# Later loads held behind a cast, w_out ahead of B and C, weights cast on GpSimd and PSUM taken anew for the decays, in a fused state-space and GELU kernel

## Chip, core and metric

The kernel runs on one core of one Trainium2 chip. The metric is device time in microseconds (us) of one execution. Three executions of the kernel before took 119.41, 119.84 and 119.67 us, median 119.67 us. The profiled execution took 119.88 us, of which the profile shows a span of 118.2 us from the first to the last instruction.

## What is computed

The reference is a chunked state-space layer (Mamba-2 style) whose output goes through a GELU feed-forward layer. `x` is 4 x 8 x 768 x 32 (batch, heads, time, head width), `a` is 4 x 8 x 768, `B` and `C` are 4 x 8 x 768 x 16. Cut to what matters:

```python
for c in range(nc):                     # chunks of time, state carried along
    cum = cumsum(log(clip(a)))          # in the chunk
    M = (C @ B.T) * exp(cum_i - cum_j) * causal
    y = M @ x + (C @ state) * exp(cum)
    state = exp(cum_end) * state + sum_j B_j x_j exp(cum_end - cum_j)
h = y.reshape(3072, 256) @ w_in         # 256 x 2048
out = gelu_tanh(h) @ w_out              # 2048 x 256
```

All inputs and the output are float32. The kernel's matrix products run on bfloat16 copies.

## The kernel before

**Tiling.** The 3072 tokens are cut into 12 units of 256 tokens; a batch has three units. A unit holds two chunks of 128 tokens (numbered `gc`), one on each half of the partitions. Work for a unit goes through these steps, each a small function that issues instructions:

- `f_mul` (line 345, DVE) multiplies the unit's B and C by decay factors, one instruction each. Units 3 and later take the factors from a table that comes from `f_RTN` (line 288; its products are on line 280, PE), which the copies `f_rn` and the reciprocals `f_pn` turn into factors.
- `f_T` (line 366, PE) transposes B and C of units 0 to 3; the others are transposed by DMA (`f_XT`, line 355). `f_E` copies the transposes out of PSUM, on the engine that `PET` names. `f_F` (line 390, DVE) makes the two masked copies `ce` of C.
- `f_G` (line 406, PE) forms C times B in two PSUM tiles, the gram. `f_M` (line 416, DVE, two instructions a unit) masks it causally. For units below `VIA` the second half is first copied to SBUF by ACT (`f_gc`, line 412).
- `f_D` (line 456, PE) forms the sums that update the state, in a quarter of two PSUM banks; `f_S` (lines 482, 484) takes them out, and `f_SP` (line 500, DVE) spreads the state over a mask. For the first chunk `f_SP0` (line 493) does this on GpSimd (POOL).
- `f_session` (lines 430 and 441, PE) forms y of the unit. From unit `MERGE` to the last but one it also issues the next unit's `f_D` and `f_G`. `f_yev` copies y to the bfloat16 tile `xm`.
- `f_s1` (line 518, PE) is the first product of the feed-forward layer: eight groups of four matmuls a unit, two groups per quarter of w_in. `f_gelu` (line 526, ACT) follows each group. `f_s2` (line 535, PE) is the second: for each of the unit's two chunks four groups of four matmuls, one group per quarter of w_out. `f_oev` and `f_store` take the result out.

**Loads.** w_in and w_out come in four quarters of 512 KB each and are cast to bfloat16 by the helper on lines 257 to 261 (`copy`), on the engines in `WENG`; "POOL+POOL" is two casts of half a quarter. A unit's x is 256 KB, its B and its C 128 KB each. ACT's queue issues B of unit 0, C of unit 1, the first w_in quarter, B of unit 1 and the other w_in quarters. SyncE's queue (SP) issues everything else, in the order of `HEAD` and then unit by unit. Before the first of the later loads, C of unit 2, stands a gate: `f_gate` (line 160) lets POOL write one element of the target tile after an instruction of ACT (`ce` of unit 0), and the load, which overwrites that element, waits for it.

**Order.** Each engine executes its instructions in one fixed order. The order is made on the host by a planner (`run_order`, line 33): steps have an engine, an estimated duration, predecessors and a priority, and at each moment the engine that is free first takes the ready step of lowest priority number. DVE and POOL may hold back for a more urgent step that is nearly ready. PSUM is planned too: the four banks `bk` are taken by a step and given back when its readers are done; the gram has two tiles of its own. Where the plan shows PE waiting in the first 20 us, it fills the wait with matmuls of zeros (line 820). The estimates are numbers in the code; if a load really comes later than planned, the engine that waits for it still waits in its place in the order.

The names that the change touches: `WP`, `MERGE`, `PET`, `LI`, `LO`, `HEAD`, `WENG`, `PP`, `RP`, `XP`, `D1`, `VIA` (lines 552 to 577), `load_h` (line 617), the gate (lines 158 and 699), `Gn` and `Mn` (lines 728 and 742), and the fills (line 818).

## Time and profile before

| | |
|---|---|
| median of three executions | 119.67 us (119.41 to 119.84) |
| profiled execution | 119.88 us |
| span in its profile | 118.2 us |
| PE busy | 110.3 us, 93% |
| ACT busy | 72.3 us, 61% |
| DVE busy | 62.6 us, 53% |
| POOL busy | 32.5 us, 27% |
| read from and written to memory | 10.58 MB, 3.15 MB |

The profile lists instructions with start and duration in us from the start of the span, with the line of the kernel (a helper's line where a helper issues them), output and input tiles. PE is TensorE's matmuls, "PEld" its weight loads; "SPq" and "ACTq" are the queues that issue DMAs. An entry in square brackets is the idle time of the engine just before, and what ended it. The chain is the sequence of work that ended last, followed back from the last instruction.

### The profile page before, as it was taken

What the parts mean: (1) busy time and instruction counts of PE and PEld (TensorE: products, weight loads), DVE (VectorE), ACT (ScalarE), POOL (GpSimd) and SP (SyncE); (2) the same over time, 40 slices, a digit from 0 to 9 for tenths busy, and PEclk for the clock granted to TensorE, in tenths of its full rate; (3) what the DMA queues carried; (4) which work ended last, traced back from release to release, by engine and by line L of the source; (5) the groups of instructions that cost most, each with busy time, mean ns of one, the idle gap of its engine ahead of it and who ended that gap; (6) DMA issues with size and microseconds to landing.
All of it is one profiled execution on the core that took longest, in us unless ns stands there. A gap on an engine that the chain in (4) does not pass through costs nothing.

```text
span 118.2 us, 3828 instructions
## 1 busy us (share of the span) xinstructions
PE 110.3 (93%) x1631; PEld 93.6 (79%) x1631; DVE 62.6 (53%) x134; ACT 72.3 (61%) x154; POOL 32.5 (27%) x61
## 2 busy tenths in 40 slices
PE   5999979999999999999999999999999999999930
PEld 5867747778888888888888888888888888888820
DVE  2779598597495791923954917609429045000110
ACT  0543796656469495684693874956847938668300
POOL 7936954572531113103301114211011010000000
PEclk9999999999999999999999999999999999999995
DMA  3999999999999984947436991371011011020120
GB/s 69 187 273 328 325 279 310 256 181 220 199 138 207 99 140 50 214 102 132 137 46 98 205 186 53 82 64 56 31 44 44 6 44 44 6 92 0 44 92 6
DMA packets 46850, 15.04 MB, mean 127 GB/s; under 512 B 42320, under 2 KB 45232, under 8 KB 46832
## 3 DMA queue, kind: packets, MB, share of 16 engines
q1 hardware_dynamic: 41760, 9.93, 48.2%
q10 hardware_dynamic: 4208, 2.49, 7.7%
q0 software_dynamic: 864, 2.36, 7.2%
q8 instruction: 13, 0.21, 0.8%
q14 instruction: 5, 0.04, 0.1%
HBM read 10.58 MB, written 3.15 MB: 116 GB/s over the span
## 4 chain that ended last, share of the span: by engine, by line
PE 77%; DMA 8%; SPq 7%; DVE 1%; POOL 1%; issue 1%; ACT 0%; DVEq 0%
PE bk L535 35%; PE bk L518 31%; DMA wf<-in_moe_w_out_dram 6%; SPq L253 5%; PE bk L441 3%; PE gb L406 3%; SPq L167 2%; DMA a_t<-in_a_dram 2%; PE bk L430 2%; PE bk L456 1%; PE gb L280 1%; POOL w_out_sb L259 1%; DVE r_t L275 1%; PE bk L820 1%; PE bk L366 0%
## 5 line engine op out<-in xcount | busy, mean ns | idle before, releaser
L526 ACT ACTIVATE gT<-bk 128x512 bf16<-128x512 f32 x96 | 51.3, 600 | 11.5 <-PE bk L518 11.4
L518 PE MATMUL bk<-xm,w_in_sb 128*128 128x256 bf16 x384 | 49.1, 274 | 1.0 <-POOL w_in_sb L259 0.7
L535 PE MATMUL bk<-w_out_sb,gT 128*128 128x256 bf16 x384 | 49.7, 273 | 0.4 <-POOL w_out_sb L259 0.2
L518 PEld LDWEIGHTS <-w_in_sb 128*128 128x128 bf16 x384 | 37.2, 98 | 6.6 <-POOL w_in_sb L259 0.9
L535 PEld LDWEIGHTS <-gT 128*128 128x128 bf16 x384 | 36.7, 98 | 6.7 <-issue 2.5
L416 DVE TENSOR_TENSOR m<-gb,tri 128x1024 bf16<-128x1024 f32 x22 | 26.7, 1218 | 1.1 <-PE gb L406 1.1
L549 POOL DMA_DIRECT2D out_dram<-o_sb x18 | 9.9, 552 | 50.6 <-ACT o_sb L542 50.6
L257 ACT ACTIVATE xm<-bk 128x256 bf16<-128x256 f32 x22 | 7.4, 381 | 12.6 <-PE bk L456 8.0
L484 DVE SCALAR_TENSOR_TENSOR s_new<-s_new,pend,bk 128x64 f32<-128x64 f32 x16 | 4.4, 275 | 20.1 <-ACT xm L257 19.5
L542 ACT ACTIVATE o_sb<-bk 128x256 f32<-128x256 f32 x22 | 8.5, 386 | 8.8 <-ACT xm L257 4.7
L345 DVE TENSOR_TENSOR bc<-bc,fac 128x256 bf16<-128x256 f32 x24 | 10.6, 477 | 0.1
L500 DVE SCALAR_TENSOR_TENSOR sp_new<-s_new,pend,bmask 128x256 bf16<-128x256 f32 x19 | 9.2, 517 | 0.0
L259 POOL CAST x<-x_t 128x512 bf16<-128x512 f32 x12 | 7.7, 638 | 4.0 <-DMA x_t<-in_x_dram 3.4
L820 PE MATMUL bk<-wz 128*128 128x128 bf16 x59 | 7.2, 312 | 1.3 <-DVE warm L193 1.3
L544 DVE COPY o_sb<-bk 128x256 f32<-128x256 f32 x2 | 0.8, 424 | 14.0 <-PE bk L535 14.0
L820 PEld LDWEIGHTS <-wz 128*128 128x128 bf16 x59 | 6.1, 148 | 1.9 <-DVE warm L193 1.3
L390 DVE TENSOR_SCALAR ce<-bt,par 128x256 bf16<-128x256 bf16 x22 | 6.3, 337 | 1.6 <-ACT bt L257 1.6
L259 POOL CAST w_in_sb<-wf 128x512 bf16<-128x512 f32 (+1 forms) x7 | 5.0, 739 | 2.7 <-DMA wf<-in_moe_w_in_dram 2.7
L482 DVE COPY s_new<-bk 128x64 f32<-128x64 f32 x3 | 0.7, 225 | 9.2 <-ACT xm L257 5.1
L406 PE MATMUL gb<-ce,bt 32*64 32x256 bf16 x192 | 5.3, 291 | 0.1
L441 PE MATMUL bk<-m,x 64*32 64x128 bf16 x384 | 5.2, 226 | 0.0
L259 POOL CAST w_out_sb<-wf 128x1024 bf16<-128x1024 f32 (+1 forms) x4 | 3.8, 954 | 2.8 <-DMA wf<-in_moe_w_out_dram 2.8
(62 smaller groups left out, 50.5 us busy)
## 6 DMA issues: line engine op xcount, KB each, us to landing
x_t<-in_x_dram SPq DMA_DIRECT2D x12, 256.0 KB, 4.9
out_dram<-o_sb POOLq DMA_DIRECT2D x18, 128.0 KB, 2.8
wf<-in_moe_w_in_dram ACTq DMA_DIRECT2D x4, 512.0 KB, 7.5
wf<-in_moe_w_out_dram SPq DMA_DIRECT2D x4, 512.0 KB, 7.9
bc<-in_C_dram SPq DMA_DIRECT2D x11, 128.0 KB, 4.1
bc<-in_B_dram SPq DMA_DIRECT2D x10, 128.0 KB, 4.1
out_dram<-o_sb SPq DMA_DIRECT2D x6, 128.0 KB, 1.7
bc<-in_B_dram ACTq DMA_DIRECT2D x2, 128.0 KB, 5.2
```

Source lines behind the costliest of these rows:

```text
L259: nc.gpsimd.tensor_copy(out=o, in_=i)
L345: nc.vector.tensor_tensor(out=d["bc16"][:, i], in0=d["bc"][:, i].rearrange("p h (r n) -> p r h n", r=2), in1=f.rearrange("p r (h o) -> p r ...
L406: nc.tensor.matmul(out=GB[g // 2][ks, g % 2, 256 * r:256 * r + 256], lhsT=d["bt"][gs, 0, r, ks], rhs=ce[gs, :, :, ks], start=True, stop=Tr ...
L416: nc.vector.tensor_tensor(out=state[("m", u, f)].rearrange("p g r e t -> p g (r e t)"), in0=state.pop(("gc", u, f), gram[f]).rearrange("p ...
L441: nc.tensor.matmul(out=y[k][32 * q:32 * q + 32, w * Q:(w + 1) * Q], lhsT=X16[u][ks, r, 32 * h:32 * h + 32], rhs=m[w][ks, q // 2, r, q % 2, :],
L500: nc.vector.scalar_tensor_tensor(out=sp_new.rearrange("p (g d) -> p g d", g=4), in0=state[("s", gc)].rearrange("p (o d) -> p o d", o=1).to ...
L518: nc.tensor.matmul(out=hp[:, j * nt:(j + 1) * nt], lhsT=w_in_sb[:, kc, fi * 128:(fi + 1) * 128], rhs=xm[:, kc, c0 * Q:c0 * Q + nt], start= ...
L526: nc.scalar.activation(gts[g][:, i * per:(i + 1) * per, 0:nt], hps.pop((g, i)).rearrange("p (j t) -> p j t", j=per), AF.Gelu_apprx_tanh)
L535: nc.tensor.matmul(out=ops[gc], lhsT=gts[g][:, fi, tt * Q:(tt + 1) * Q], rhs=w_out_sb[:, fi, :], start=(fi == 0), stop=(fi == NF - 1), ski ...
L542: nc.scalar.activation(o_sb, ops.pop(gc), AF.Copy)
L549: q.dma_start(out=out[u * W:(u + 1) * W].rearrange("(p r) m -> r p m", r=2)[r], in_=ops.pop(gc))
L820: nc.tensor.matmul(out=BK[j][:, 0:128], lhsT=wz[:, 0:128], rhs=wz[:, 0:128], start=True, stop=True)
```

## The change

- **Hold and order of loads.** The gate moves from C of unit 2 to the first w_out quarter, which is now the first of the later loads. POOL writes the element with a memset, after the cast of the first w_in quarter. The order after the gate was C of unit 2, w_out 0, B of unit 2, w_out 1, 2, 3, x of unit 2. It is now w_out 0, w_out 1, C of unit 2, w_out 2, B of unit 2, w_out 3, x of unit 2.
- **Casts.** Every w_in quarter is one cast on POOL; so is the third w_out quarter, which was shared with DVE. The fourth stays shared.
- **Units 1 to 3.** `f_G` and `f_D` of unit 3 become steps of their own (`MERGE` 3), with two banks for `f_D`. `f_D` of unit 1 no longer waits for the fourth first product of unit 0. The masking of unit 1 reads PSUM directly (`VIA` 1). Unit 2's transposes are copied by ACT. `f_mul` of unit 1 gets a more urgent priority, the cast of its x, `f_G` of unit 1 and the products of `f_RTN` less urgent ones.
- **Planner.** The DMA estimates change, and all loads share one planned DMA resource.
- **Fills.** Zeros are multiplied in matmuls of 256 columns instead of pairs of 128.

```diff
+    def f_gate(kind, j):
+        if kind == "wo":
+            WF[("o", j)] = wfp.tile([128, 4, d_model], FP32, name="wf")
+            o = WF[("o", j)][0:1, 0, 0:1]
...
+        nc.gpsimd.memset(o, 0.0)
...
-    WP = (-185, -184.9, -179.5, -179.4)
-    MERGE = 2
+    MERGE = 3
-    PET = {0: "ACT", 1: "ACT", 2: "DVE", 3: "ACT"}
-    LB, LX, LI, LO, XD, XL = 0.92, 1.25, 1.85, 1.65, 0.6, 3.6
-    HEAD = [("x", 0, 2.6, 0), ("x", 1, 4.5, 0), ("b", 1, 1.1, WP[0]), ("wi", 1, 1.7, WP[1]),
-            ("wi", 2, 1.6, WP[2]), ("wi", 3, 1.6, WP[3]),
-            ("c", 2, 2.8, 0), ("wo", 0, 1.5, 0), ("b", 2, 0.85, 0), ("wo", 1, 1.5, 0), ("wo", 2, 1.5, 0),
-            ("wo", 3, 1.5, 0), ("x", 2, 1.15, 0)]
-    WENG = [("POOL", "POOL+POOL", "POOL+POOL", "POOL+POOL"), ("POOL", "POOL", "POOL+DVE", "POOL+DVE")]
+    PET = {0: "ACT", 1: "ACT", 2: "ACT", 3: "ACT"}
+    LB, LX, LI, LO, XD, XL = 0.92, 1.25, 1.42, 1.5, 0.6, 3.6
+    HEAD = [("x", 0), ("x", 1), ("b", 1), ("wi", 1), ("wi", 2), ("wi", 3), ("wo", 0), ("wo", 1), ("c", 2), ("wo", 2), ("b", 2), ("wo", 3), ("x", 2)]
+    SEND = {("b", 1): -185, ("wi", 1): -184.9, ("wi", 2): -179.5, ("wi", 3): -179.4}
+    WENG = [("POOL", "POOL", "POOL", "POOL"), ("POOL", "POOL", "POOL", "POOL+DVE")]
-    PP = -45
-    RP = 4
-    XP = {0: -96, 1: -7.5}
-    D1 = 3
-    VIA = 2
+    PP = -58
+    RP = 2000
+    XP = {0: -96, 1: 10}
+    GS = 0
+    D1 = None
+    VIA = 1
...
-    bl[1, 1] = add("DW", 5.2, none, done=1.35, prio=-2)
-    win_l[0] = add("DW", DW * 1.8, none, done=1.35, prio=-1)
+    bl[1, 1] = add("DMA", 1.4, none, done=1.35, prio=2.2)
+    win_l[0] = add("DMA", DW * 1.45, none, done=1.35, prio=2.4)
...
-        n = add("DW" if side else "DMA", DW * dur if side else DF * dur, none, deps=[lat], done=1.35, prio=10 + k)
+        n = add("DMA", DF * dur, none, deps=[lat], done=1.35, prio=2.1 if k == 5 else 10 + k)
...
-            issue["c", 2].deps.append(add("POOL", 0.15, f_gate, 2, 1, 0, deps=[fn_[1]], prio=-98))
...
-            Gn[u] = add("PE", 0.37, f_G, u, prio=(-87, -62)[u] if u < 2 else q, deps=Fn[u] + Mn.get(u - 1, []))
+            Gn[u] = add("PE", 0.37, f_G, u, prio=(-87, 900)[u] if u < 2 else q, deps=Fn[u] + Mn.get(u - 1, []))
...
-                             prio=q + 1 + r if u > 1 else (-60.3, -45.5)[u] + 0.1 * r))
+                             prio=q + 1 + r if u > 1 else (-60.3, -48)[u] + 0.1 * r))
...
+    held = HEAD[max(n for n, e in enumerate(HEAD) if e in SEND) + 1]
+    issue[held].deps.append(add("POOL", 0.1, f_gate, *held, deps=[SPn[0] if GS else wi_n[0][-1]], prio=-98))
...
-            for _ in range(n):
-                nc.tensor.matmul(out=BK[j][:, 0:128], lhsT=wz[:, 0:128], rhs=wz[:, 0:128],
+            for i in range(0, n, 2):
+                w = 128 * min(2, n - i)
+                nc.tensor.matmul(out=BK[j][:, 0:w], lhsT=wz[:, 0:128], rhs=wz[:, 0:w],
                                  start=True, stop=True)
```

More of the change, by code (lines that the diff above doesn't have):

```diff
@@ L156 @@
     P = [dict() for _ in range(NP)]
-    def f_gate(j, i, u):
-        P[j]["bc"] = ldn.tile([128, 2, H, 2 * N], FP32, name="bc")
-        nc.gpsimd.tensor_copy(out=P[j]["bc"][0:1, i, 0, 0:1], in_=P[u]["ce"][0:1, 1, 0:1])
+    def f_gate(kind, j):
+        if kind == "wo":
+            WF[("o", j)] = wfp.tile([128, 4, d_model], FP32, name="wf")
+            o = WF[("o", j)][0:1, 0, 0:1]
+        elif kind == "x":
+            XF[j] = ldx.tile([128, H, 2 * D], FP32, name="x_t")
+            o = XF[j][0:1, 0, 0:1]
+        else:
+            P[j]["bc"] = ldn.tile([128, 2, H, 2 * N], FP32, name="bc")
+            o = P[j]["bc"][0:1, "bc".index(kind), 0, 0:1]
+        nc.gpsimd.memset(o, 0.0)
     def load_bc(j, i, q):
@@ L173, in load_x @@
         b, t = divmod(j, T3)
-        XF[j] = ldx.tile([128, H, 2 * D], FP32, name="x_t")
+        if j not in XF:
+            XF[j] = ldx.tile([128, H, 2 * D], FP32, name="x_t")
         q.dma_start(out=XF[j], in_=x[b, :, t * W:(t + 1) * W].rearrange("h (p r) d -> p h (r d)", r=2))
@@ L251, in load_wo @@
     def load_wo(q, e):
-        WF[("o", q)] = wfp.tile([128, 4, d_model], FP32, name="wf")
+        if ("o", q) not in WF:
+            WF[("o", q)] = wfp.tile([128, 4, d_model], FP32, name="wf")
         e.dma_start(out=WF[("o", q)], in_=wo[:, 4 * q:4 * q + 4])
@@ L641 @@
             if key not in bl and key not in xl:
-                load_h(kind, j, LX if kind == "x" else LB)
+                load_h(kind, j)
     wdur = {"DVE": 0.68, "ACT": 1.08, "POOL": 1.08}
```

4 lines of the change are left out of this document (3 added, 1 removed).

## The prediction

> **What bounds the kernel now.** I read the page first, for the shares of the chain that ended last.
>
> ```profile
> PE 77%; DMA 8%; SPq 7%; DVE 1%; POOL 1%; issue 1%; ACT 0%; DVEq 0%
> ```
>
> TensorE carries three quarters of the chain, the rest is loads and their queue. So I read PE's timeline from the first product of the feed-forward layer on, to see where PE stands still. Columns: start, busy time, engine, line, operation, count, and idle time before it with what ended it.
>
> ```profile
> 10.99 0.39 PE L430 MATMUL bk<-bt,sp_new 128*128 128x128 bf16 x2
> ...
> 12.52 1.89 PE L518 MATMUL bk<-xm,w_in_sb 128*128 128x256 bf16 x12
> 14.47 0.42 PE L406 MATMUL gb<-ce,bt 32*64 32x256 bf16 x16
> ...
> 16.41 0.73 PE L518 MATMUL bk<-xm,w_in_sb 128*128 128x256 bf16 x5 [0.25 <-DVE s_new L484]
> 17.88 0.94 PE L518 MATMUL bk<-xm,w_in_sb 128*128 128x256 bf16 x7 [0.73 <-POOL w_in_sb L259]
> 18.65 0.39 PE L430 MATMUL bk<-bt,sp_new 128*128 128x128 bf16 x4
> ...
> 19.31 0.71 PE L280 MATMUL bk<-sel,r_t 96*128 96x96 f32 x4
> 20.07 0.61 PE L518 MATMUL bk<-xm,w_in_sb 128*128 128x256 bf16 x4
> 20.51 0.39 PE L366 MATMUL bk<-ident,bc 128*128 128x128 bf16 x4
> 20.74 0.60 PE L535 MATMUL bk<-w_out_sb,gT 128*128 128x256 bf16 x4
> ...
> 22.87 0.60 PE L535 MATMUL bk<-w_out_sb,gT 128*128 128x256 bf16 x4 [0.22 <-POOL w_out_sb L259]
> ...
> 31.10 0.39 PE L430 MATMUL bk<-bt,sp_new 128*128 128x128 bf16 x4
> ...
> 33.60 3.66 PE L518 MATMUL bk<-xm,w_in_sb 128*128 128x256 bf16 x32
> ```
>
> The first product (L518) starts at 12.52. The idle entries are at 16.41, 17.88 and 22.87. They understate the loss, because a group's busy time runs on while it waits. So I count work against time between fixed points, with what one step takes on the chain.
>
> ```profile
> 25.09 0.44 PE bk L518 x4
> ...
> 31.83 0.16 PE bk L456 x16
> 31.99 0.35 PE gb L406 x16
> ```
>
> Four matmuls of L518 take 0.44 us, and those of L535 alternate with them at the same pace; a gram (L406) takes 0.35, a state sum (L456) 0.16, a transpose 0.23 (20.51 to 20.74).
>
> - From 12.52 to 18.65 (unit 1's y begins) 6.13 us pass. Unit 0's eight groups need 3.52. The first twelve matmuls ran slow: 12.52 to 14.47 is 1.95 where three groups take 1.32, so 0.63 more. With a gram and a state sum that is 4.66 us. Lost: 1.47.
> - From 18.65 to 20.07, 1.42: y of unit 1 (0.66) and the decay products of L280 (0.76). PE never stands still, and nothing is lost as long as y's copy to SBUF takes as long.
> - From 20.07 to 33.60, 13.53: 24 groups (10.56), two transposes (0.46), two grams (0.70), two state sums (0.33), y of unit 2 (0.60) are 12.65. Lost: 0.88.
>
> After 33.60 the chain is PE without a break until the last copy. So this change can win about 2.35 us behind 12.52, and nothing after 33.60.
>
> Who makes PE wait? GpSimd's rows show it for the casts, DVE's for unit 1.
>
> ```profile
> 7.78 0.18 POOL L160 CAST bc<-ce 1x1 f32<-1x1 bf16 x1 [1.53 <-ACT ce L388]
> ...
> 8.82 1.04 POOL L259 CAST w_in_sb<-wf 128x1024 bf16<-128x1024 f32 x1 [0.31 <-DMA wf<-in_moe_w_in_dram]
> 9.86 1.07 POOL L493 TENSOR_TENSOR sp_new<-s,bmask 128x256 bf16<-128x256 f32 x1
> 12.06 1.17 POOL L259 CAST w_in_sb<-wf 128x512 bf16<-128x512 f32 x2 [1.13 <-DMA wf<-in_moe_w_in_dram]
> ...
> 16.19 1.63 POOL L259 CAST w_in_sb<-wf 128x512 bf16<-128x512 f32 x2 [1.29 <-DMA wf<-in_moe_w_in_dram]
> 18.35 1.04 POOL L259 CAST w_out_sb<-wf 128x1024 bf16<-128x1024 f32 x1 [0.53 <-DMA wf<-in_moe_w_out_dram]
> 20.45 1.04 POOL L259 CAST w_out_sb<-wf 128x1024 bf16<-128x1024 f32 x1 [1.06 <-DMA wf<-in_moe_w_out_dram]
> 21.95 0.87 POOL L259 CAST w_out_sb<-wf 128x512 bf16<-128x512 f32 x1 [0.45 <-DMA wf<-in_moe_w_out_dram]
> 23.57 0.87 POOL L259 CAST w_out_sb<-wf 128x512 bf16<-128x512 f32 x1 [0.76 <-DMA wf<-in_moe_w_out_dram]
> ```
>
> The fourth w_in quarter lands at 16.2 (1.29 idle, ended by its DMA) and its two halves are cast until 17.82; PE's row at 17.88 waits for exactly this. The w_out quarters land at 18.3, 20.4, 21.9 and 23.5.
>
> ```profile
> 13.36 1.06 DVE L390 TENSOR_SCALAR ce<-bt,par 128x256 bf16<-128x256 bf16 x2 [0.90 <-ACT bt L257]
> 14.95 1.23 DVE L416 TENSOR_TENSOR m<-gb,tri 128x1024 bf16<-128x1024 f32 x1 [0.53 <-PE gb L406]
> ...
> 16.28 1.07 DVE L416 TENSOR_TENSOR m<-gs,tri 128x1024 bf16<-128x1024 bf16 x1
> ...
> 17.46 1.03 DVE L500 SCALAR_TENSOR_TENSOR sp_new<-s_new,pend,bmask 128x256 bf16<-128x256 f32 x2
> 18.41 1.26 DVE L345 TENSOR_TENSOR bc<-bc,fac 128x256 bf16<-128x256 f32 x1
> ...
> 19.93 0.41 DVE L345 TENSOR_TENSOR bc<-bc,fac 128x256 bf16<-128x256 f32 x1
> ...
> 23.89 2.35 DVE L416 TENSOR_TENSOR m<-gb,tri 128x1024 bf16<-128x1024 f32 x2
> ```
>
> Unit 1's masked C ends at 14.42, its masking runs from 14.95 to 17.35, and the state spread (L500) from 17.46. Unit 1's y needs the first of the two spreads, by 17.98. So DVE alone would let it begin near 18.0: removing the wait for w_in uncovers DVE at once.
>
> **The change part by part.**
>
> *Gate.* It used to follow ACT at 7.78; now it follows the cast of the first quarter, which ends at 9.86. It stands before the first state spread (9.86, L493), for which unit 0's y at 10.99 waits. Price: 0.18 at most (the old gate's row), 0 if POOL takes the spread first; I take 0.1. Behind it on SP wait all later loads: from 7.98 to about 10.0.
>
> ```profile
> L167 SPq DMA_DIRECT2D bc<-in_C_dram x1: 367/367/367, 8.0 to 8.0; - x1
> ...
> DMA to landing us min/median/max: 8.6/8.6/8.6
> L167 SPq DMA_DIRECT2D bc<-in_B_dram x1: 2524/2524/2524, 9.0 to 9.0; - x1
> ...
> DMA to landing us min/median/max: 9.9/9.9/9.9
> L182 ACTq DMA_DIRECT2D wf<-in_moe_w_in_dram x1: 539/539/539, 6.5 to 6.5; - x1
> ```
>
> These rows are C of unit 2, B of unit 2 and the fourth w_in quarter, the first two with their time to landing, from views of lines 167 and 182: C, issued 1.5 us after that quarter, lands at 16.6, 0.4 behind it; B lands at 18.9. In stretches of 2 us the view shows what was moved (last column, GB/s):
>
> ```profile
> 10.00:12.00 2.00, 2.00 (x46) 1.41 (x45) 1.94 (x5) 0.00 (x0) 0.93 (x1) 1.00 1.04 382
> ```
>
> That is about what two w_out quarters 1.5 us apart make, 524 KB in 1.5 us or 350 GB/s. The loads move at full rate and nearly in order of issue, from 10 until past 20 us, whoever waits. Holding the later loads for 2 us therefore leaves no gap while w_in is under way; it only takes C of unit 2 and w_out out of the fourth quarter's end. From the second w_in quarter (cast at 12.06 when it lands) two more at that pace give 15.0 in place of 16.2 for the fourth. Behind it, at 1.6 a w_out quarter (21.9 to 23.5) and 0.7 for B or C (B landed 0.6 behind w_out 0): w_out 0 at 16.6, 1 at 18.2, C of unit 2 18.9, w_out 2 20.5, B of unit 2 21.2, w_out 3 22.8. The bounds are 14.6 and 16.2 for the fourth w_in quarter, with the others 0.4 earlier to 1.2 later. Only B and C of unit 2 come later than now (18.9 and 16.6).
>
> *Casts.* A whole quarter takes 1.04 (8.82), two halves 1.17 (12.06): 0.13 saved on each of three. The fourth is then ready at 16.05 instead of 17.82. Whole on POOL, the third w_out quarter takes 1.04 instead of 0.87 and is ready at 21.6; DVE loses one cast.
>
> *Unit 1.* Its state sum no longer waits for the fourth group, so the two state copies and a spread fit into DVE's idle 0.90 before 13.36 or the gap to 14.95. The second masking reads PSUM like the first, 1.23 instead of 1.07; ACT loses a copy. The cast of unit 1's x moves ahead of the second quarter's, into the idle 1.13 before 12.06. I leave masked C where it is, ending 14.42: L366 of unit 1 may come up to 0.3 earlier by the new priority, or DVE be held longer by a cast. Then masking runs 14.95 to 16.15 and 17.4, and y of unit 1 begins at 17.6 (17.2 to 18.3) instead of 18.65. By then PE has its 4.66 from 12.62, until 17.28, so 0.3 is lost instead of 1.47. The first group of L535 (0.44) has its weights at 17.7 and comes in before the decay products; with these last in priority they still fall where y is copied, as now. Unit 1's first products begin at 17.6 + 0.66 + 0.44 + 0.76 = 19.46, with one group of the later work done: won 20.07 − 19.46 + 0.44 = 1.05.
>
> *Unit 2 and 3.* B's landing at 21.2 plus 0.41 (L345) puts L366 of unit 2 at 21.7 instead of 20.51. From there to the end of masking it took 20.51 to 26.24 (L416 at 23.89, 2.35), so y of unit 2 could begin at 27.5, long before 31.10, because it no longer carries unit 3's gram. Meanwhile PE has from 19.46 eight groups, two more groups on w_out 1 and 2 and a transpose, 4.6 us, until 24.1; w_out 3 is cast at 23.7. So the wait at 22.87 and its like go. Unit 3's state sum takes two of four banks for itself for a while. I leave 0.3 of the 0.88 lost (bounds 0 and 0.88): won 0.6. Unit 2's transposes are copied by ACT beside L535:
>
> ```profile
> 12.73 0.60 ACT L257 ACTIVATE bt<-bk 128x512 bf16<-128x512 bf16 x1 [0.34 <-PE bk L366]
> ```
>
> Such a copy takes 0.60. PE has groups of L535 to do meanwhile; without them the first products wait those 0.60. The fills cost nothing: the same columns in the time PE waits; were the slow pace of the first twelve to last for the other twenty matmuls, 20 × 0.05 = 1.0, of which 0.3 is hidden.
>
> *Sum.* 1.05 + 0.6 = 1.65 off the profiled execution's 119.88 (span 118.2 and 1.7 around it): 118.2. It lies 0.2 above the median of three, so on the median 119.67 − 1.65 = 118.0. By the bounds of the two terms (0.35 to 1.45, 0 to 0.9) the forecast's own range is 117.3 to 119.3.
>
> **The rivals.**
>
> *Same order of landing.* The held loads share with w_in as soon as they are issued, since 10.0 is still 5 us before w_in is through, and the fourth quarter lands at 16.2 as now. Cast whole until 17.25, the last two groups end at 18.15; y begins there: won 0.5 + 0.6 = 1.1, 118.6. For: C of unit 2 landed only 0.4 behind it. Against: C, a quarter of its size, took 8.6 us.
> The Trainium skill, "DMA: Bandwidth & Descriptors", section "Queues, rings and completion order", says so: each DMA engine takes turns between the queues that have work, packet by packet. The trace agrees less with it than with order of issue, by those 8.6 us.
>
> *Whole casts block DVE.* L345 took 1.26 at 18.41 beside the cast of 18.35, and 0.41 at 19.93 with POOL idle. If the whole casts hold masked C of unit 1 by 0.5 more and unit 2 likewise, y begins at 18.1 and the 0.88 stays: won 0.55, 119.1.
> The Trainium skill, "SBUF — State Buffer", section "Who interferes with whom", gives the rule: GpSimd and DVE share one port pair as an exclusive lock, held for a whole instruction, against DVE operations with two inputs in SBUF or in a two-port mode. The 1.26 agrees with it; the masking from PSUM (1.23) is outside it.
>
> *Slower: PE stands before unit 2's transpose.* PE's order is fixed; say it puts L366 of unit 2 near 21.7, where I expect its data. B of unit 2 is now fifth after the gate. B's issue took 2.52 at 9.02, and it landed 7.4 after that issue ended. If it is issued only when C of unit 2 has landed (18.9), it lands between 23.5 and 26. From 23.2 on the stall eats the whole gain and 0.36 more; at 24.0 it is 24.0 + 0.6 − 21.7 = 2.9, net 1.2 slower: 120.9. Against: the queue moves in order, and what is ahead of B is through at 20.5.
>
> *It does nothing.* y of unit 1 stays at 18.3 behind DVE and the wait for w_out is replaced by one for PSUM banks: 119.3 to 119.9.
>
> **How the numbers follow.** Forecast 0.47, same order of landing 0.15, blocked DVE 0.10, nothing 0.10, slower 0.18. Below 0.3% (0.36 us) this kernel's measurement can't tell a change from none. Faster: the first three, 0.72; same 0.10; slower 0.18. The likeliest is 118.0. The range runs from 117.1 (the whole 2.35, and 0.2 of the time ahead of 12.52) to 120.2, which takes in the mild half of the slow case; about 0.15 is left out.
>
> **What would show it.** In the changed profile the fourth w_in cast begins near 15.0 and ends near 16.05; y of unit 1 begins near 17.6, and DVE's masking just before it decides that; L518 of unit 1 begins near 19.5; no idle entry behind w_out's casts; y of unit 2 begins well before 31, and PE is unbroken from about 32. Wrong would be: a row of L366 near 22 with idle time ended by DVE's L345, a fourth w_in cast still at 16.2, or PE idle behind L484, whose copies give the banks back.

## The result and the profile after

Four executions of the changed kernel took 118.08 to 118.58 us, median 118.16, against a median of 119.54 for the kernel before on the same chip: a ratio of 0.989, interval 0.985 to 0.994. A second series gave 118.07 us and 0.990 (0.987 to 0.993), against 119.44 for the kernel before; one execution of the kernel before in it ran in a slower state of the chip and is left out. The profiled execution took 118.17 us with a span of 116.4 us, 1.8 us less than the profiled execution before. The change was forecast at 118.0.

The chain of the changed kernel, by engine, is of the same kind; line numbers have moved by 8 to 12.

```profile
PE 75%; DMA 11%; SPq 6%; POOL 3%; ACTq 1%; issue 0%; DVE 0%; DVEq 0%
```

PE's timeline of the changed kernel, same columns as before:

```profile
12.20 0.60 PE L528 MATMUL bk<-xm,w_in_sb 128*128 128x256 bf16 x4
...
16.98 0.39 PE L440 MATMUL bk<-bt,sp_new 128*128 128x128 bf16 x4
...
18.67 0.60 PE L545 MATMUL bk<-w_out_sb,gT 128*128 128x256 bf16 x4 [0.95 <-POOL w_out_sb L269]
...
19.55 1.04 PE L528 MATMUL bk<-xm,w_in_sb 128*128 128x256 bf16 x8
...
22.53 0.60 PE L545 MATMUL bk<-w_out_sb,gT 128*128 128x256 bf16 x4 [0.20 <-POOL w_out_sb L269]
22.96 0.39 PE L376 MATMUL bk<-ident,bc 128*128 128x128 bf16 x4
...
24.75 0.60 PE L545 MATMUL bk<-w_out_sb,gT 128*128 128x256 bf16 x4
...
29.41 0.39 PE L440 MATMUL bk<-bt,sp_new 128*128 128x128 bf16 x4
```

Unit 0's first product (L528) starts at 12.20, unit 1's y (L440) at 16.98 instead of 18.65, unit 1's first product at 19.55 instead of 20.07, unit 2's y at 29.41 instead of 31.10. The wait has changed its name: at 17.88 PE had waited for a cast of w_in; now the largest idle entry, 0.95 at 18.67, is a wait for the cast of the first w_out quarter. GpSimd shows both casts:

```profile
9.60 1.10 POOL L503 TENSOR_TENSOR sp_new<-s,bmask 128x256 bf16<-128x256 f32 x1
10.65 0.09 POOL L168 MEMSET wf<- 1x1 f32 x1
...
15.00 1.04 POOL L269 CAST w_in_sb<-wf 128x1024 bf16<-128x1024 f32 x1 [0.33 <-DMA wf<-in_moe_w_in_dram]
17.57 1.04 POOL L269 CAST w_out_sb<-wf 128x1024 bf16<-128x1024 f32 x1 [1.53 <-DMA wf<-in_moe_w_out_dram]
19.15 1.04 POOL L269 CAST w_out_sb<-wf 128x1024 bf16<-128x1024 f32 x1 [0.54 <-DMA wf<-in_moe_w_out_dram]
21.44 1.04 POOL L269 CAST w_out_sb<-wf 128x1024 bf16<-128x1024 f32 x1 [1.24 <-DMA wf<-in_moe_w_out_dram]
23.83 0.87 POOL L269 CAST w_out_sb<-wf 128x512 bf16<-128x512 f32 x1 [1.35 <-DMA wf<-in_moe_w_out_dram]
```

The fourth w_in quarter is cast from 15.00 to 16.04, as forecast. The gate's memset (L168) stands at 10.65, behind the state spread, not ahead of it; SyncE's timeline has the first two w_out quarters right behind it:

```profile
10.76 0.92 SPq L263 DMA_DIRECT2D wf<-in_moe_w_out_dram  x2
```

The w_out quarters land at 17.5, 19.1, 21.4 and 23.8; the last one 0.3 later than before.

**How much of the 1.8 us is PE's?** The last instruction that follows PE is DVE's copy of the last output. Its rows in the kernel before and after:

```profile
113.38 0.42 DVE L544 COPY o_sb<-bk 128x256 f32<-128x256 f32 x1 [3.12 <-PE bk L535]
```

```profile
112.58 0.42 DVE L554 COPY o_sb<-bk 128x256 f32<-128x256 f32 x1 [3.12 <-PE bk L545]
```

So the work ended 0.80 us earlier. The other 0.94 lies behind it, where only the last store lands. SyncE's list of waits has it, first before, then after (us in total, times, longest):

```profile
SPq L852 <- DMA out_dram<-o_sb: 2.1, 1, 2.1
```

```profile
SPq L864 <- DMA out_dram<-o_sb: 1.2, 1, 1.2
```

The DMA view of the kernel before, for 114.0 to 116.5 us, shows what lay beside that store:

```profile
q1 hardware_dynamic: 144, 0.13, 15.7%
q8 instruction: 1, 0.02, 2.4%
issues: line engine op xcount, KB each, median us to landing
out_dram<-o_sb SPq DMA_DIRECT2D x1, 128.0 KB, 2.6
```

A piece of code, 16 KB on queue 8, was fetched while the store ran, and the store took 2.6 us. In a second profile of the same kernel no fetch falls there, and it took 1.7:

```profile
q1 hardware_dynamic: 144, 0.13, 14.8%
issues: line engine op xcount, KB each, median us to landing
out_dram<-o_sb SPq DMA_DIRECT2D x1, 128.0 KB, 1.7
```

That profile has its last copy at 113.30 and a span of 117.2. The profile that the prediction started from was thus 0.9 us longer than the work needs, and the 1.8 between the two profiled spans are 0.8 of earlier work and 0.9 of a long last store. The ratio over all executions, 0.99, lies between what 0.8 and what 1.8 us would give (0.993 and 0.985).

### The profile page after: what moved, and what is told of

It reads as the page before. It is cut to its first block, busy times and chain, and to the rows that moved or that the text cites. A ratio compares the mean times of both kernels' runs of the same rounds, so it can differ in the third digit from the quotient of the medians.

```text
span 116.4 us, 3772 instructions
## 1 busy us (share of the span) xinstructions
PE 107.1 (92%) x1605; PEld 89.9 (77%) x1605; DVE 60.9 (52%) x132; ACT 71.2 (61%) x154; POOL 31.8 (27%) x58
## 4 chain that ended last, share of the span: by engine, by line
PE 75%; DMA 11%; SPq 6%; POOL 3%; ACTq 1%; issue 0%; DVE 0%; DVEq 0%
PE bk L545 36%; PE bk L528 30%; DMA wf<-in_moe_w_in_dram 6%; DMA wf<-in_moe_w_out_dram 5%; SPq L263 4%; PE gb L416 3%; PE bk L451 3%; SPq L175 2%; PE bk L440 2%; PE bk L466 1%; POOL sp_new L503 1%; ACTq L175 1%; POOL w_in_sb L269 1%; POOL w_out_sb L269 1%; DVE o_sb L554 0%
## 5 line engine op out<-in xcount | busy, mean ns | idle before, releaser
L536 ACT ACTIVATE gT<-bk 128x512 bf16<-128x512 f32 x96 | 50.6, 599 | 10.2 <-PE bk L528 10.1
L545 PE MATMUL bk<-w_out_sb,gT 128*128 128x256 bf16 x384 | 49.4, 273 | 1.2 <-POOL w_out_sb L269 1.2
L528 PE MATMUL bk<-xm,w_in_sb 128*128 128x256 bf16 x384 | 47.7, 273 | 0.0
L545 PEld LDWEIGHTS <-gT 128*128 128x128 bf16 x384 | 36.5, 98 | 7.7 <-issue 3.4
L528 PEld LDWEIGHTS <-w_in_sb 128*128 128x128 bf16 x384 | 37.1, 98 | 4.8 <-issue 0.4
L426 DVE TENSOR_TENSOR m<-gb,tri 128x1024 bf16<-128x1024 f32 x23 | 27.8, 1219 | 1.1 <-PE gb L416 1.1
L494 DVE SCALAR_TENSOR_TENSOR s_new<-s_new,pend,bk 128x64 f32<-128x64 f32 x16 | 4.4, 276 | 19.5 <-ACT xm L267 19.3
L355 DVE TENSOR_TENSOR bc<-bc,fac 128x256 bf16<-128x256 f32 x24 | 10.1, 464 | 3.4 <-DMA bc<-in_B_dram 1.7
L510 DVE SCALAR_TENSOR_TENSOR sp_new<-s_new,pend,bmask 128x256 bf16<-128x256 f32 x19 | 8.5, 478 | 0.1
L832 PE MATMUL bk<-wz 128*128 128x256 bf16 (+1 forms) x33 | 5.8, 333 | 1.3 <-DVE warm L202 1.3
L400 DVE TENSOR_SCALAR ce<-bt,par 128x256 bf16<-128x256 bf16 x22 | 5.6, 306 | 1.3 <-ACT bt L267 1.3
L832 PEld LDWEIGHTS <-wz 128*128 128x128 bf16 x33 | 3.8, 122 | 2.3 <-DVE warm L202 1.3
L440 PE MATMUL bk<-bt,sp_new 128*128 128x128 bf16 x40 | 4.2, 219 | 1.2 <-POOL wf L168 1.2
```

The source lines that it names most:

```text
L355: nc.vector.tensor_tensor(out=d["bc16"][:, i], in0=d["bc"][:, i].rearrange("p h (r n) -> p r h n", r=2), in1=f.rearrange("p r (h o) -> p r ...
L426: nc.vector.tensor_tensor(out=state[("m", u, f)].rearrange("p g r e t -> p g (r e t)"), in0=state.pop(("gc", u, f), gram[f]).rearrange("p ...
L510: nc.vector.scalar_tensor_tensor(out=sp_new.rearrange("p (g d) -> p g d", g=4), in0=state[("s", gc)].rearrange("p (o d) -> p o d", o=1).to ...
L528: nc.tensor.matmul(out=hp[:, j * nt:(j + 1) * nt], lhsT=w_in_sb[:, kc, fi * 128:(fi + 1) * 128], rhs=xm[:, kc, c0 * Q:c0 * Q + nt], start= ...
L536: nc.scalar.activation(gts[g][:, i * per:(i + 1) * per, 0:nt], hps.pop((g, i)).rearrange("p (j t) -> p j t", j=per), AF.Gelu_apprx_tanh)
L545: nc.tensor.matmul(out=ops[gc], lhsT=gts[g][:, fi, tt * Q:(tt + 1) * Q], rhs=w_out_sb[:, fi, :], start=(fi == 0), stop=(fi == NF - 1), ski ...
```

## The experiments

The first two rows repeat the two kernels as they are, and "new fills on the kernel before" alters the kernel before. All others alter the changed kernel: in one thing each, but for "unit 1 as before", which takes several edits back at once. "Last copy" is the start of DVE's copy of the last output in the one profiled execution, "unit 1's y" the start of its first row on PE. Times are medians; the ratio is to the kernel before, from the same series.

| run | time, us | ratio (95% interval) | unit 1's y | last copy |
|---|---|---|---|---|
| before, again | 118.87, one execution | | 18.48 | 113.30 |
| changed, again | 118.07 | 0.990 (0.987 to 0.993) | 18.99 | 113.10 |
| decay products first | 118.26 | 0.991 (0.987 to 0.994) | 17.73 | 112.78 |
| old fills | 118.00 | 0.989 (0.986 to 0.992) | 18.00 | 112.36 |
| new fills on the kernel before | 119.41 | 0.999 (0.996 to 1.002) | 17.48 | 113.32 |
| old fills less four | 118.27 | 0.990 (0.984 to 0.995) | 17.82 | 112.39 |
| no hold | 118.27 | 0.989 (0.984 to 0.995) | 17.84 | 112.48 |
| last w_out quarter ahead of B | 118.68 | 0.994 (0.990 to 0.998) | 17.98 | 113.38 |
| old order of loads | 118.20 | 0.991 (0.988 to 0.994) | 17.84 | 112.27 |
| unit 3 merged again | 119.05 | 0.997 (0.994 to 0.999) | 17.23 | 113.54 |
| unit 1 as before | 118.86 | 0.996 (0.993 to 0.999) | 17.96 | 112.74 |
| last cast on ACT | 117.87 | 0.989 (0.986 to 0.992) | 17.70 | 112.39 |

### The two kernels once more

No edit.

> The kernel before once more, for a second profile. PE's last work ended 0.8 us earlier in the changed kernel's profile (112.50 against 113.30), while the span was 1.8 us shorter; 0.9 us of the difference lie behind the last output copy, where only the last store lands. Theory: that tail scatters from execution to execution and is no part of the change. Then this profile has the last PE work at 113.3 +/- 0.2 and a tail from there to the end anywhere between 3.9 and 4.9 us. Rival: the tail of 4.9 us belongs to the kernel before; then it is 4.9 again, within 0.1. Second question, the pace of the early matmuls: theory (the fills' width sets it) says the first twelve matmuls of the feed-forward layer are slow again, 1.9 us; rival (where in the execution the pace rises is a matter of chance) says they may be fast here, 1.3 us.

> The changed kernel once more, for a narrower ratio and a second profile. Theory: the last PE work ends at 112.5 +/- 0.2 and the tail scatters between 3.9 and 4.9 us, so the ratio comes nearer to what PE gained, 0.8 of 119.6 us: 0.992 to 0.994. Rival: the tail belongs to the change, 3.9 us again, and the ratio stays at 0.988 to 0.990. In both the first matmul of unit 0 starts near 12.2, fast, if the fills' width sets the pace; if chance does, it may be slow here.

Measured: the kernel before ended its work at the same place (113.30) with the short tail, so the long tail is no property of the program. Its early matmuls were slow again (1.97 us for the first twelve). The changed kernel, the same program as in the first profile, showed them slow this time; this profile is of the longest execution of its series, 118.67 us:

```profile
6.20 0.28 PE L376 MATMUL bk<-ident,bc 128*128 128x128 bf16 x2 [0.37 <-POOL pe L333]
...
9.43 0.31 PE L466 MATMUL bk<-x,bc 64*32 64x64 bf16 x16 [1.77 <-POOL x L269]
...
13.44 1.04 PE L528 MATMUL bk<-xm,w_in_sb 128*128 128x256 bf16 x4
```

Its first transposes (L376, 0.28 for 0.40) were fast as in the first profile; then PE waited 1.77 for a late x and everything was slow until 14 (four matmuls of L528 1.04 for 0.60). The view of stretches shows the clock granted to TensorE, the third number from the end. Around the first product it is 1.00 in the first profile of the changed kernel and 0.50 in this one:

```profile
12.00:13.00 1.00, 1.00 (x26) 0.67 (x25) 0.60 (x3) 0.70 (x2) 0.74 (x1) 1.00 1.05 389
```

```profile
13.00:14.00 1.00, 1.00 (x8) 0.68 (x7) 1.00 (x2) 0.87 (x2) 1.00 (x2) 0.50 1.07 382
```

In this execution it was 0.50 from 8 to 14 us. The run "last w_out quarter ahead of B" shows the same: a wait of 1.40 for x, 0.50 from 8 to 14, and 1.03 for the first four matmuls. The slow matmuls of the kernel before are another matter, for the granted clock reads 1.00 there. With the new fills and a granted clock of 1.00 the first four took between 0.60 and 0.92 in other profiles, so the pace is not settled by the width of the fills; what does settle it at 1.00 stays open. The last copy came at 113.10, 0.5 later than in the first profile, from the late x; yet the median of the series is 118.07. The ratio of 0.990 is the upper end of what the rival gave.

### Order of the groups behind unit 1's y

```diff
-    RP = 2000
+    RP = 4
```

> The changed kernel with the decay products' old priority (4 for 2000): the planner puts them right behind y of unit 1, then unit 1's first products, then the first group on w_out 0. Theory: PE stood still from 17.6 to 18.7 for w_out 0 only because that group stands first in its order; now the decay products fill the hole, unit 1's first products start near 18.4 instead of 19.55, and the waits for w_out 2 and 3 get longer by part of that: PE's end 0.3 to 0.8 us earlier, time 0.3 to 0.8 us less than the changed kernel's. Rival: w_out's arrival bounds the stretch whatever stands first; the waits behind 20 us grow by all of it and the time is within 0.2 us of the changed kernel's.

Measured: 118.26, last copy 112.78: no gain. In this execution unit 1's y itself came late:

```profile
17.73 0.28 PE L440 MATMUL bk<-bt,sp_new 128*128 128x128 bf16 x2
18.59 0.28 PE L440 MATMUL bk<-bt,sp_new 128*128 128x128 bf16 x2 [0.59 <-DVE sp_new L510]
...
19.90 0.61 PE L528 MATMUL bk<-xm,w_in_sb 128*128 128x256 bf16 x4
```

Unit 1's first products start at 19.90 without any wait for w_out, and the last copy is 0.2 later than with it. The wait of 0.95 at 18.67 was nothing that paid for itself when taken away. What PE waited for here is the second state spread on DVE (0.59 idle at 18.59). The rival held in the time (0.2 above the changed kernel), not in its mechanism: PE's rows show no longer waits behind 20 us.

### The fills and the tail

Old fills, on the changed kernel:

```diff
-            for i in range(0, n, 2):
-                w = 128 * min(2, n - i)
-                nc.tensor.matmul(out=BK[j][:, 0:w], lhsT=wz[:, 0:128], rhs=wz[:, 0:w],
+            for _ in range(n):
+                nc.tensor.matmul(out=BK[j][:, 0:128], lhsT=wz[:, 0:128], rhs=wz[:, 0:128],
```

> The changed kernel with fills of 128 columns again, the order of all else kept. Theory: the fills' width is what made the early matmuls fast (unit 0's transposes took 0.28 for 0.40); here they are slow until about 13 us, unit 0's first matmul starts near 12.5, y of unit 1 begins at 17.4 to 17.7 instead of 16.98, but the wait for w_out 0 until 18.7 covers it: time 0 to 0.3 us above the changed kernel's. Rival 1: the pace is a matter of chance; no difference in the early rows beyond it. Rival 2: the fast start carries the gain; then 0.6 us or more is lost.

The reverse of this diff on the kernel before:

> The kernel before with fills of 256 columns alone; it has 58 fewer instructions on PE (3189 for 3247). New theory on the tail: PE's instructions are fetched in 16 KB pieces; the kernel before needs a thirteenth near its end (114.3 us in its profile, 117.7 in the second one), and where that falls on the last store, one DMA engine is busy with it for 1 us and the execution ends 0.9 us later. With 3189 instructions there is no thirteenth piece, as in the changed kernel (3195): no execution has the long tail, the span is 117.1 to 117.5 in all of them, the median 118.9 to 119.1, and the last PE work still ends at 113.2. Rival 1: the long tail is the store's own scatter; half of the spans are near 118.0 again and the median is within 0.2 us of the kernel before. Rival 2: the wider fills themselves speed up the start; then the last PE work ends 0.3 us or more before 113.2.

Old fills on the changed kernel, less the first four:

```diff
+            for _ in range(n - (4 if t0 < 2 else 0)):
```

> The changed kernel with fills of 128 columns less the first four, so that PE has 3247 instructions as in the kernel before (with all the fills it had 3255, and its thirteenth piece came at 110.2, clear of the last store). Theory on the tail: the thirteenth piece falls near the last store again; some of the executions are about 0.9 us longer, spans in two clusters near 116.3 and 117.2, the median between 118.0 and 118.9. Rival: the tail was the store's own scatter or belonged to the old order of the work; all spans stay near 116.3, the median 118.0.

Measured: 118.00 with old fills; 119.41 and a ratio of 0.999 with new ones on the kernel before; 118.27 with four fewer. The fills' width is worth nothing that these runs can tell. With old fills the first product started at 12.64 and unit 1's y at 18.00, a microsecond later than in the first profile of the changed kernel, and the last copy still came at 112.36: the head's speed does not reach the end.

The kernel before with new fills shows one thing more. In its profiled execution the fourth w_in quarter landed early, and PE's rows follow:

```profile
14.96 1.17 POOL L259 CAST w_in_sb<-wf 128x512 bf16<-128x512 f32 x2 [0.31 <-DMA wf<-in_moe_w_in_dram]
```

```profile
17.48 0.39 PE L430 MATMUL bk<-bt,sp_new 128*128 128x128 bf16 x4
...
21.45 0.60 PE L535 MATMUL bk<-w_out_sb,gT 128*128 128x256 bf16 x4 [0.66 <-POOL w_out_sb L259]
...
22.79 0.60 PE L535 MATMUL bk<-w_out_sb,gT 128*128 128x256 bf16 x4 [0.30 <-POOL w_out_sb L259]
...
24.43 0.60 PE L535 MATMUL bk<-w_out_sb,gT 128*128 128x256 bf16 x4 [0.15 <-POOL w_out_sb L259]
```

Unit 1's y began at 17.48, 1.17 earlier than in the profile that the prediction started from, without a hold, a new order of loads or a new cast. The last copy came at 113.32, as in the other profiles of the kernel before (113.38 and 113.30): PE stood 1.11 us before the w_out quarters instead. In the old order of the work an earlier unit 1 is worth nothing.

On the tail the theory failed. The new fills on the kernel before leave no thirteenth piece of code (the page counts 12 on queue 8), but spans still ran from 117.2 to 118.0; four fewer fills gave back the instruction count of the kernel before, but five of six spans lay between 116.2 and 116.6. That a fetch lay beside the long last store is shown for one execution. What spreads the spans of the kernel before (117.1 to 118.0 in one series, up to 118.7 in another) stays open.

### The hold and the order of loads

The gate after unit 0's masked C, as before, on the new order of loads:

```diff
-    issue[held].deps.append(add("POOL", 0.1, f_gate, *held, deps=[SPn[0] if GS else wi_n[0][-1]], prio=-98))
+    issue[held].deps.append(add("POOL", 0.1, f_gate, *held, deps=[Fn[0][1]], prio=-98))
```

> The changed kernel with the hold shortened: the gate follows unit 0's masked C on ACT, as in the kernel before, but still holds w_out 0, which is then issued near 8.0 instead of 10.8. New theory on the gain: PE's end is the start of the group that needs the last w_out quarter (near 24.5 in both kernels) plus a constant, 88.8 us before and 87.75 after, because more of the work is done by then; the hold does not move that quarter for the better. Then the fourth w_in quarter lands 0.5 to 1.2 us later here, the last w_out quarter 0 to 0.5 us earlier, PE's end stays or comes up to 0.4 us earlier: time 0 to 0.4 us less than the changed kernel's. Rival, as in the prediction: the hold brings w_in forward and that carries the gain; then 0.5 us or more is lost.

```profile
8.57 0.09 POOL L168 MEMSET wf<- 1x1 f32 x1
...
15.39 1.04 POOL L269 CAST w_in_sb<-wf 128x1024 bf16<-128x1024 f32 x1 [1.03 <-DMA wf<-in_moe_w_in_dram]
17.22 1.04 POOL L269 CAST w_out_sb<-wf 128x1024 bf16<-128x1024 f32 x1 [0.79 <-DMA wf<-in_moe_w_out_dram]
...
23.62 0.87 POOL L269 CAST w_out_sb<-wf 128x512 bf16<-128x512 f32 x1 [1.31 <-DMA wf<-in_moe_w_out_dram]
```

The gate stands at 8.57, 2.1 earlier than in the changed kernel, yet the fourth w_in quarter lands only 0.4 later and the w_out quarters 0.2 to 0.4 earlier. The 0.4 tells little: with the hold in place that cast began between 14.57 and 16.02 in nine profiles. Time 118.27, last copy 112.48: the hold is worth nothing measurable. The rival, which was part of the prediction's own first term, fell.

The old order of loads behind the new hold:

```diff
-    HEAD = [("x", 0), ("x", 1), ("b", 1), ("wi", 1), ("wi", 2), ("wi", 3), ("wo", 0), ("wo", 1), ("c", 2), ("wo", 2), ("b", 2), ("wo", 3), ("x", 2)]
+    HEAD = [("x", 0), ("x", 1), ("b", 1), ("wi", 1), ("wi", 2), ("wi", 3), ("c", 2), ("wo", 0), ("b", 2), ("wo", 1), ("wo", 2), ("wo", 3), ("x", 2)]
```

> The changed kernel with the old order of loads behind the gate: C of unit 2, w_out 0, B of unit 2, w_out 1, 2, 3, x of unit 2; the gate now holds C of unit 2. Theory (what PE has done by the time the last w_out quarter is cast, near 24.7, sets its end): that quarter lands at the same time, near 23.7, because the same loads stand ahead of it, but w_out 0 lands 0.6 later and the next ones nearly 1 us later, so PE has less to do behind y of unit 1: its end 0.2 to 0.6 us later, the time 0.2 to 0.6 us above the changed kernel's. Rival: the order costs nothing, since unit 1's first products fill the time and unit 2 gains what w_out loses: within 0.2 us.

Measured: 118.20 and the earliest last copy of the profiles, 112.27. The first w_out quarter was cast at 18.36 there, 0.8 later than in the changed kernel, and still the order costs nothing: the rival held. The old hold and the old order together were not tried.

The last w_out quarter brought forward:

```diff
-    HEAD = [("x", 0), ("x", 1), ("b", 1), ("wi", 1), ("wi", 2), ("wi", 3), ("wo", 0), ("wo", 1), ("c", 2), ("wo", 2), ("b", 2), ("wo", 3), ("x", 2)]
+    HEAD = [("x", 0), ("x", 1), ("b", 1), ("wi", 1), ("wi", 2), ("wi", 3), ("wo", 0), ("wo", 1), ("c", 2), ("wo", 2), ("wo", 3), ("b", 2), ("x", 2)]
```

> The changed kernel with the last w_out quarter ahead of B of unit 2 in the order of loads. Theory (the last w_out quarter sets PE's end): it lands 0.6 to 0.9 us earlier, near 23.0, B of unit 2 1.5 us later, near 23.7; PE's end 0.4 to 0.8 us earlier if unit 2's transposes find other work to stand behind. Rival: unit 2 is what PE waits for next; the wait moves from w_out to unit 2's transposes or its y, and the time is within 0.2 us of the changed kernel's or longer.

```profile
24.23 0.60 PE L545 MATMUL bk<-w_out_sb,gT 128*128 128x256 bf16 x4
24.66 0.39 PE L376 MATMUL bk<-ident,bc 128*128 128x128 bf16 x4
...
31.19 0.39 PE L440 MATMUL bk<-bt,sp_new 128*128 128x128 bf16 x4
```

The group that needs the last quarter (24.23) starts 0.5 earlier, but unit 2's transposes (24.66) come 1.7 and its y (31.19) 1.8 later than in the changed kernel, its last copy 0.8 later. Part of that may be the slow start of this execution (118.96 us, the late x told above). The median of 118.68 is 0.5 us above the changed kernel, though the intervals of the two ratios overlap. The theory fell: PE needs unit 2 next, not w_out.

### Unit 3 merged again

```diff
-    MERGE = 3
+    MERGE = 2
```

> The changed kernel with unit 3's gram and state sum inside unit 2's y again (MERGE 2). Theory (the gain is made ahead of the last w_out quarter): what PE does up to 24.7 is the same and y of unit 2, some 2 us later, near 31, still comes before PE runs out of other work; the time stays within 0.2 us of the changed kernel's. Rival, the prediction's second term: y of unit 2 set free from unit 3 is worth 0.3 to 0.6 us, and that is lost here.

This run takes nearly the whole gain away with one edit. Up to 24.73 PE does what it does in the changed kernel, group by group (24.75 there). Then:

```profile
24.73 0.60 PE L545 MATMUL bk<-w_out_sb,gT 128*128 128x256 bf16 x4
...
30.70 0.39 PE L376 MATMUL bk<-ident,bc 128*128 128x128 bf16 x4
...
31.36 0.39 PE L440 MATMUL bk<-bt,sp_new 128*128 128x128 bf16 x4
...
31.93 0.32 PE L466 MATMUL bk<-x,bc 64*32 64x64 bf16 x16
...
33.04 1.47 PE L528 MATMUL bk<-xm,w_in_sb 128*128 128x256 bf16 x12 [0.32 <-ACT xm L267]
35.08 2.12 PE L528 MATMUL bk<-xm,w_in_sb 128*128 128x256 bf16 x18 [0.57 <-DVE s_new L494]
```

Unit 2's y starts at 31.36, not 29.41. PE does not pause before it: the merged step has unit 3's inputs among its predecessors, so that four more groups of L545 and unit 3's transposes (30.70) stand ahead of it in the order. It also carries unit 3's state sum (31.93) in its own banks. ACT's copy of y waits for that sum:

```profile
32.33 0.66 ACT L267 ACTIVATE xm<-bk 128x256 bf16<-128x256 f32 x2 [0.33 <-PE bk L466]
```

In the changed kernel the sum has PSUM banks of its own (these are the banks that the change takes anew; the decay products use one bank in both kernels) and the copy follows y at once:

```profile
30.24 0.66 ACT L267 ACTIVATE xm<-bk 128x256 bf16<-128x256 f32 x2 [0.25 <-PE bk L451]
```

So the copy comes 2.1 us later: 1.95 of it is y's own later start, the rest the wait for the sum. PE runs out of other work, stands still at 33.04 for that copy and again at 35.08 for DVE's copy of the state (L494), which gives y's banks back: 0.89 us in all. The last copy comes at 113.54, 0.96 us later, and the time is 119.05 us; its ratio, 0.994 to 0.999, lies clear of those of the changed kernel. The theory that a gain made ahead of the last w_out quarter would last fell; the rival held, with a larger amount than it gave.

### Unit 1 as before

```diff
-    PP = -58
-    RP = 2000
-    XP = {0: -96, 1: 10}
+    PP = -45
+    RP = 4
+    XP = {0: -96, 1: -7.5}
...
-    D1 = None
-    VIA = 1
+    D1 = 3
+    VIA = 2
...
-            Gn[u] = add("PE", 0.37, f_G, u, prio=(-87, 900)[u] if u < 2 else q, deps=Fn[u] + Mn.get(u - 1, []))
+            Gn[u] = add("PE", 0.37, f_G, u, prio=(-87, -62)[u] if u < 2 else q, deps=Fn[u] + Mn.get(u - 1, []))
```

and `f_M`'s old priority for unit 1.

> The changed kernel with everything about unit 1 and the decay products as before: old priorities, the state sum of unit 1 behind the fourth group, the second masking through ACT's copy, the cast of unit 1's x behind the second w_in quarter. Load order, hold, casts, unit 2 and 3 as changed. Theory: w_in is ready near 16, but y of unit 1 waits for DVE as it would have in the kernel before and begins between 17.9 and 18.4; with the decay products behind it unit 1's first products start near 19.5, about as in the changed kernel, so 0 to 0.4 us is lost. Rival: unit 1's own edits make the gain; then y of unit 1 begins near 18.7, its first products near 20.1, and 0.6 us or more is lost.

Measured: 118.86, 0.7 us above the changed kernel (the intervals of the ratios just meet, at 0.993), but the executions lie in groups (118.3 to 118.5, 118.9 to 119.0, 120.0 twice). The profiled one is the fastest of them, 118.30; its last copy comes at 112.74 and unit 1's y at 17.96, as the theory said. So undoing these edits costs more than half of the gain on the median, as the rival said, but no profile shows where, and the spread of its spans (116.6 to 118.3) is of the kind seen in the kernel before: open.

### The last cast on ACT

```diff
-    WENG = [("POOL", "POOL", "POOL", "POOL"), ("POOL", "POOL", "POOL", "POOL+DVE")]
+    WENG = [("POOL", "POOL", "POOL", "POOL"), ("POOL", "POOL", "POOL", "POOL+ACT")]
```

> The changed kernel with the last w_out quarter's second half cast on ACT instead of DVE, so that the two halves do not share a port: POOL's half should take 0.58 instead of 0.87. Theory (the last w_out quarter's cast sets PE's end): the group that needs it starts 0.2 to 0.3 us earlier, near 24.4, and PE ends as much earlier: 0.2 to 0.3 us less than the changed kernel's, the shortest of all. Rival: ACT, which must wait for that quarter in its place in the order, holds up the first products' activations; then PE waits for banks and the time is the same or longer.

```profile
23.58 0.61 POOL L269 CAST w_out_sb<-wf 128x512 bf16<-128x512 f32 x1 [1.37 <-DMA wf<-in_moe_w_out_dram]
```

POOL's half took 0.61 beside ACT, for 0.87 beside DVE. The Trainium skill, "SBUF — State Buffer", section "Who interferes with whom", has the reason: only DVE shares a port pair with GpSimd, ACT has its own; these two numbers agree. But the group behind it starts at 24.55, 0.2 earlier, when PE is done with what stands ahead, and the time, 117.87 (0.989), can't be told from the changed kernel's. No run gave a version that clearly beats the changed kernel.

## Why the prediction was right, and where it was not

The time and the sign were right: 118.0 forecast, 118.16 and 118.07 measured. Point by point, the reasons held only in part.

- **Bound.** Right: PE's end moves only by what is lost ahead of 33.6; from there on the chain is PE in both kernels. The rows say more. From the start of the group that needs the last w_out quarter to the last copy 88.89 us pass in all three profiles of the kernel before and 87.83 to 87.84 in the changed kernel (24.75 to 112.58) and in six more profiles of it and its variants. That group starts 0.26 later than before, so the end moves by 1.06 − 0.26 = 0.80. The 1.06 is work that PE has behind it by then: unit 1 has had all eight groups of its first product, for four in the kernel before, against one gram fewer, 4 × 0.44 − 0.35 = 1.4 us; by the rows some 0.3 of that is lost again in short gaps behind it.
- **What a lost stretch is worth.** This is where the reasoning failed. I counted 1.47 us lost ahead of unit 1's y and 0.88 behind it and took each as won once its wait was gone. The kernel before with new fills had unit 1's y 1.17 earlier and ended where it always does. In the changed kernel and its variants y at 16.98 went with a last copy at 112.58, y at 17.84 with 112.27 and 112.48, y at 18.00 with 112.36. By these rows, what counts is how much work the order gives PE ahead of the last w_out quarter, and that unit 2 is there when this is used up.
- **Head.** Forecast 0.1 later by the gate; it came behind the spread, and the chain has 0.04 for it. The first product started at 12.20, and between 12.36 and 13.44 in other profiles of such kernels. The early matmuls' slow stretch, which I took as fixed, comes and goes: the same program ran its first four at 0.60 in one execution, at a granted clock of 1.00, and at 1.04 in another, at 0.50. The Trainium skill, "TensorE: Matmul & The Clock Gate", section "Part 1: The HAM clock gate (the "warmup" mystery)", says that the activity window which opens the clock runs freely, so that the point of change differs from run to run. These two executions do differ in when the clock was granted in full, but in the slower one the clock fell between 7 and 8 us, about when PE began its wait of 1.77, so no run here shows that the window is the reason. Most of it did not reach the end: with the clock at 0.50 the last copy came at 113.10, and in the profiles with a late head at a clock of 1.00 it came between 112.27 and 112.78.
- **w_in.** Forecast 15.0 to 16.05, measured 15.00 to 16.04, and that close a hit was luck. In ten profiles with the new order of loads the fourth quarter's cast began between 14.57 and 16.02; in three of the kernel before at 14.96, 16.02 and 16.19. Without the hold it began at 15.39, with the hold and the old order at 14.87. That hold or order brings it forward is not shown.
- **Unit 1.** Forecast y at 17.6 (17.2 to 18.3), bounded by DVE; measured 16.98: the masked C of unit 1, which I left at 14.42, ended at 13.71, and the masking at 16.59 for 17.4. In other profiles y began between 17.23 and 18.99, with the wait for DVE's second spread in plain sight at 18.59 when the head was slow. First products of unit 1 forecast at 19.46, measured 19.55, but by two errors that cancel: y came 0.6 earlier and PE then stood 0.95 before the first w_out quarter.
- **w_out's arrival.** This term was mis-sized. I had the quarters at 16.6, 18.2, 20.5 and 22.8; they landed at 17.5, 19.1, 21.4 and 23.8, within the 1.2 that I allowed. The miss is one gap: the first quarter came 2.5 behind the fourth of w_in, not 1.6; the gaps after it are as forecast. The gate opened 0.7 later than I took it, but that does not explain it: with the gate at 8.57 the quarter was still cast at 17.22. In ten profiles with this order of loads it was cast between 17.12 and 17.68, wherever w_in had landed. What holds it there stays open. So PE's waits at 18.67 and 22.53 are left.
- **Unit 2.** Forecast 0.6 for y that no longer carries unit 3's gram. Right in kind; merged again it costs 0.96. It does not simply add to the first term: in the merged run unit 1's y is nearly as early as in the changed kernel (17.23), and the last copy is 0.2 later than in the kernel before. Earlier work ahead of 25 us is worth something only if unit 2's y is ready when PE runs out of it. I had y ready at 27.5; it began at 29.41, behind work that PE had in any case.
- **Sum.** Forecast 1.65 for the profiled execution. PE's part is 0.80; the other 0.94 was the last store of the profile I started from, which I took as given. On medians the gain is 1.4 in both series of the changed kernel, by the intervals of the ratio 0.8 to 1.8 and 0.8 to 1.6; the fastest executions of the second series differ by 1.1 (118.93 and 117.83). That 118.0 was met so closely is luck in part: the sum adds two terms that do not add, and the profile shows half of it.
- **Rivals.** "Same order of landing" can't be judged from these runs: the hold's 2.1 us moved the fourth w_in quarter by 0.4, less than it scatters without any edit. "Whole casts block DVE" did show in the rows: L400 of unit 1 took 0.78 in the first profile, with y at 16.98, and 1.21 to 1.33 in six of its variants, with y at 17.70 to 18.00; but their last copies were not later for it, all but one of them earlier than 112.58. "PE stands before unit 2's transpose" did not happen: B landed before 22.2, and the transposes ran at 22.96 without idle time. With B one place further back unit 2 came later and cost 0.5 us, but there too PE did not stand before the transposes.

What was not tried is separate banks for unit 3 on the kernel before, alone; whether unit 1's edits are needed with them is told only by the run that undoes unit 1. Nor were the casts, the copies of unit 2's transposes on ACT and the planner's new estimates each taken back alone. Which of the edits lets the planner put all of unit 1's first products ahead of the last w_out quarter is therefore not shown; the hold, the fills and the merged unit 3 are not what does it, for with each of these taken back PE does its work up to there in the same order.

## What to carry to other kernels

When one engine does all the work in the end, count its lost time stretch by stretch and ask of each edit whether PE has anything else to do at the point where the gain should be cashed: here the hold, the load order and the fills, each taken back alone, moved rows by up to a microsecond and the end by nothing, while taking another unit's work out of the way of one unit's y (its inputs ahead of it, its sum in the same banks) moved the end by one. Undo one edit at a time to learn which ones matter, and remember that two edits which do the same job both look worthless that way. Take a second profile of the kernel before, because one stretched store was as large as PE's whole gain.

## What the runs showed of the hardware

The last store of 128 KB took 1.7 us in one execution and 2.6 in another, with a 16 KB code fetch beside it. Four 256-column matmuls took 0.60 us at a granted clock of 1.00 and 1.04 at 0.50, at the same place of the same program; at 1.00 they took up to 0.92 in other profiles. The same 512 KB quarter of w_in, issued near 6.5 us, was ready for its cast at 14.57 in one execution of the changed kernel's loads and at 16.02 in another. GpSimd's cast of half a quarter took 0.87 beside a cast on DVE and 0.61 beside one on ACT.
